# Reordered opening loads, one warm-up moved and a two-piece tail in a fused linear-attention and token-mixing kernel

## The chip, the cores and the metric

The kernel runs on one core of a Trainium2 chip. The metric is the device time of one execution in microseconds, the median of several runs. Engines are named as in the profile: PE is the matmul engine and PEld its weight loads, DVE the vector engine, ACT the scalar engine, POOL the GpSimd engine, SP the engine that issues most transfers. A transfer (DMA) is issued by SP, ACT or POOL into that engine's own queue.

## The reference

Two branches over the same `x` of 2048 rows (S) by 512 columns (D), mixed by a gate per row. `_A_ref` is linear attention with 32 heads of 16 columns, `_B_ref` an MLP over the rows (tokens).

```python
g = sigmoid((x * gate_w).sum(-1))
# A: linear attention
q, k, v = split(x @ wqkv)                      # heads of 16
pq, pk = phi(q), phi(k)                        # phi(t) = where(t > 0, t + 1, exp(t)) + 1e-6
kv = pk^T v ; z = sum_s pk                     # per head
a = ((pq kv) / (pq z + 1e-6)) @ wo
# B: MLP across tokens
h = layernorm(x)
u = gelu(einsum("bsd,sf->bdf", h, w1) + b1)    # F = 1792
b = (u @ w2 + b2)^T
out = g * a + (1 - g) * b
```

Inputs and output are bf16.

## The kernel before

The 2048 rows are 16 tiles of 128 (index `t`), the 512 columns 4 chunks of 128 (index `k` or `j`), F is 14 blocks of 128. `xs` holds x as it is, `xT` its transpose, `wk_sb` the key part of `wqkv` as 4 chunks of 128 rows, each 128 KB. The schedule is manual: each engine executes its instructions in the order of the program text, so the text's order is the queue's order on every engine.

The stages, in order:

- **Opening.** The loads of x tile 0, x tile 1 and the four chunks of Wk are issued, three on SP and two on ACT. Behind them SP issues transposing loads that fill `xT` for the tiles from 2 on, then x, Wq, W1, Wv, Wo. Meanwhile PE runs `warm_up(6)`: six matmuls of 512 columns on a constant, into a bank `wps` that nobody reads. For tiles 0 and 1 (`HEADS = 2`) the transpose is made on PE: `transpose_part` multiplies 128x128 pieces of `xs` by the identity into a bank `pt`, and `copy_part` copies them to `xT` on DVE (line 205 of the profile) or ACT (line 203). Each tile has three parts: chunk 0, chunk 1, chunks 2 and 3. `k_part(t, ks)` then adds steps `ks` of the four accumulation steps of K for tile t, into the bank `kacc`; step k needs `xT` chunk k of that tile and Wk chunk k. PE's order is: transposes of tile 0, steps 0 and 1 of tile 0, transposes of tile 1, step 2 of tile 0, steps 0 and 1 of tile 1, step 3 of tile 0, steps 2 and 3 of tile 1.
- **K loop.** For tiles 2 to 15: four `kacc` steps, `phi` (ACT exp at line 209, DVE at 210 and 213) into `pk`, and with a lag of 4 tiles the Gram products `gacc` (`x^T pk`). Layer-norm statistics run beside it.
- **Q and first W1 blocks.** 16 rounds of three `uacc` matmuls (line 110, as for all matmuls) with the first W1 chunk `w1c[0]`, and one `q_block` of four.
- **Rest of W1.** 11 more F blocks, 16 matmuls each, with gelu; small matmuls for kv and W2; normalisation of q on DVE.
- **Output loop.** For each row tile, 4 `aps` matmuls and 14 `yps` matmuls over the F blocks, one ACT scaling (line 488), one DVE combination (line 501) into `ot`, and a store (line 505). The last row tile is cut by columns into pieces of 256, 128 and 128, each with its own 14 matmuls, combination and store.

The code of the opening's loads and of the tail:

Of the kernel before, what the change touches and what calls it, by code (L numbers as in the profile page):

```python
# [15 lines left out]
def kernel(  # L16
# [13 lines left out]
    nc = tc.nc  # L30
    P = nc.NUM_PARTITIONS
# [6 lines left out]
    S, D = X.shape  # L38
    F = B_w1.shape[1]
    NT = S // P  # L40
# [16 lines left out]
    w1_view = B_w1.rearrange("(t p) f -> p t f", p=P)  # L57
# [11 lines left out]
    def bank(name, dtype=FP32):  # L69
        return ps.tile([P, SC], dtype, name=name, tag="bank")  # L70
# [38 lines left out]
    def mm(o, lhsT, rhs, start, stop, **kw):  # L109
        nc.tensor.matmul(o, lhsT=lhsT, rhs=rhs, start=start, stop=stop, **kw)  # L110
# [14 lines left out]
    def load_x(q, t0, n):  # L125
        q.dma_start(out=xs[:, t0 : t0 + n, :], in_=x_view[:, t0 : t0 + n, :])

    def load_wk(q, k, n):
        q.dma_start(out=wk_sb[:, k : k + n, :], in_=wqkv_view[:, k : k + n, D : 2 * D])
# [4 lines left out]
        )  # L134

    load_x(nc.sync, 0, 1)
    load_wk(nc.scalar, 0, 2)
    load_x(nc.sync, 1, 1)
    load_wk(nc.scalar, 2, 1)
    load_wk(nc.sync, 3, 1)  # L140
    for t in (2, 3, 4):
        load_xT(t, 1)
    nc.vector.memset(ones_f[:], 1.0)
# [3 lines left out]
        out=ident[:], in_=ident[:], compare_op=ALU.not_equal, fill=1.0, base=0,  # L147
# [5 lines left out]
        out=maskQ[:], in_=maskH[:].rearrange("p (a m) -> p m a", m=2), op=ALU.max, axis=AX.X  # L153
# [12 lines left out]
    for c, (j0, nb) in enumerate(w1_chunks):  # L166
        w = wpool.tile([P, NT, FB * P], BF16, name="w1c", tag="wc")
        w1c.append(w)
        nc.sync.dma_start(out=w[:, :, : nb * P], in_=w1_view[:, :, j0 * P : (j0 + nb) * P])
        if c == 0:  # L170
            nc.sync.dma_start(out=wv_sb[:], in_=wqkv_view[:, :, 2 * D : 3 * D])
            nc.sync.dma_start(out=wo_sb[:], in_=wo_view)
# [11 lines left out]
    def warm_up(n, cols=SC):  # L184
        for _ in range(n):
            mm(wps[:, :cols], warm[:, 0:P], warm[:, :cols], True, True)

    act_warm = keep([P, 1], FP32, "act_warm")
    nc.scalar.activation(out=act_warm[:], in_=ones_f[:], func=ACT.Exp)
    warm_up(6)  # L190

    pts = {}

    def transpose_part(t, k0, k1):
        pt = pts[t, k0, k1] = bank("pt")
        for k in range(k0, k1):
            mm(pt[:, k * P : (k + 1) * P], xs[:, t, k * P : (k + 1) * P], ident[:], True, True)

    def copy_part(t, k0, k1, on_act):
        src = pts.pop((t, k0, k1))[:, k0 * P : k1 * P].rearrange("p (k s) -> p k s", k=k1 - k0)  # L200
        dst = xT[:, k0:k1, t * P : (t + 1) * P]
        if on_act:
            nc.scalar.activation(out=dst, in_=src, func=ACT.Copy)
        else:
            nc.vector.tensor_copy(out=dst, in_=src)  # L205
# [13 lines left out]
    def k_part(t, ks):  # L219
        if t not in kaccs:  # L220
            kaccs[t] = bank("kacc")
        for k in ks:
            mm(
                kaccs[t][:], xT[:, k, t * P : (t + 1) * P], wk_sb[:, k, :],
                k == 0, k == ND - 1,
            )

    def k_phi(t):
        phi(pk[:, t, :], kaccs.pop(t))
# [52 lines left out]
    for t in range(HEADS):  # L282
        for k0, k1 in ((0, 1), (1, 2), (2, ND)):
            transpose_part(t, k0, k1)
            copy_part(t, k0, k1, (t, k0) in ((0, 2), (1, 1)))
        k_part(0, range(2) if t == 0 else (2,))
    k_part(1, range(2))
    k_part(0, (3,))
    k_phi(0)
    k_part(1, range(2, ND))  # L290
    k_phi(1)
# [91 lines left out]
    def den_block(c, j):  # L383
        seg = pqT[:, j, c * SC : (c + 1) * SC]
        pz = work.tile([P, SC], FP32, name="pz", tag="pz", bufs=2)
        nc.scalar.activation(out=pz[:], in_=seg, func=ACT.Copy, scale=zcol[:, j : j + 1])  # L386
        nc.vector.transpose(out=zT[:], in_=pz[:])  # L387
        den = work.tile([P, SC // HEAD], FP32, name="den", tag="den", bufs=1)
        nc.vector.tensor_reduce(  # L389
            out=den[:], in_=zT[:].rearrange("p (a d) -> p a d", d=HEAD), op=ALU.add, axis=AX.X  # L390
        )
        rd = work.tile([P, SC // HEAD], BF16, name="rd", tag="rd", bufs=1)
        with nc.allow_low_precision(reason="the normalizer is used in bf16"):
            nc.vector.reciprocal(out=rd[:], in_=den[:])
        rex = work.tile([P, SC], BF16, name="rex", tag="rex", bufs=1)
        nc.vector.transpose(  # L396
            out=rex[:].rearrange("p (a d) -> p a d", d=HEAD),
            in_=rd[:].unsqueeze(2).to_broadcast([P, SC // HEAD, HEAD]),
        )
        nc.vector.tensor_tensor(out=seg, in0=seg, in1=rex[:], op=ALU.mult)  # L400
# [42 lines left out]
    for j in range(NB0, NF):  # L443
        c, jj = divmod(j, FB)
        i = j - NB0
        acc = bank("uacc")
        for t in range(NT):
            if i == 2 and t < BRIDGE:
                for q in range(0, P, Q32):
                    c0 = jj * P + q  # L450
# [24 lines left out]
        out=gg[:], in0=gth[:], scalar1=0.5, scalar2=0.5, op0=ALU.mult, op1=ALU.add  # L475
    )
    nc.vector.tensor_scalar(
        out=c1[:], in0=gth[:], scalar1=-0.5, scalar2=0.5, op0=ALU.mult, op1=ALU.add
# [3 lines left out]
    for t in range(NT):  # L482
        c, tl = divmod(t, TPC)
        aps = bank("aps")
        for j in range(ND):
            mm(aps[:], pqT[:, j, t * P : (t + 1) * P], W2sb[:, j, :], j == 0, j == ND - 1)
        a_sc = work.tile([P, D], FP32, name="a_sc", tag="a_sc", bufs=2)
        nc.scalar.activation(  # L488
            out=a_sc[:], in_=aps[:], func=ACT.Identity,
            scale=gg[:, t : t + 1], bias=c2[:, t : t + 1],  # L490
        )
        for c0, W in ((0, 2 * P), (2 * P, P), (3 * P, P)) if t == NT - 1 else ((0, D),):
            cs = slice(c0, c0 + W)
            yps = bank("yps")
            for f in range(NF):
                mm(
                    yps[:, :W], w2c[c][:, f, tl * P : (tl + 1) * P], uT[:, f, cs],
                    f == 0, f == NF - 1,
                )
            ot = opool.tile([P, D], BF16, name="ot", tag="ot")  # L500
            nc.vector.scalar_tensor_tensor(  # L501
                out=ot[:, :W], in0=yps[:, :W], scalar=c1[:, t : t + 1], in1=a_sc[:, cs],
                op0=ALU.mult, op1=ALU.add,
            )
            (nc.scalar if t < 2 else nc.sync).dma_start(out=o_view[:, t, cs], in_=ot[:, :W])
        if t < NSC * ND - NDB:
            den_block(*divmod(t + NDB, ND))
# [30 lines left out]
```

## Time and profile before

| | |
|---|---|
| runs, us | 162.9, 163.17, 162.28 (median 162.9) |
| profiled execution, us | 162.26, its span 160.6 |
| PE busy | 155.9 us (97%), 822 matmuls |
| DVE busy | 124.3 us (77%) |
| ACT busy | 72.7 us (45%) |
| PE clock granted | 1.0 |
| HBM read, written | 19.01 MB, 2.10 MB |
| first matmul, first K matmul, last DVE combination | 0.85, 4.06, 157.82 us |

The span runs from the first to the last instruction; the execution's own time lies 1.66 us above it. Times inside the execution are in us from the span's start, durations of one instruction in ns. Matmuls are pipelined: one of 512 columns is shown as 379 ns, but a new one starts every 0.216 us. A busy share is an average over stages, and a wait is put down to what came last.

### The profile page before, as it was taken

To read this page: it belongs to the slowest core of one execution; us is meant where nothing else is said; L and a number is where in the kernel's file an instruction comes from. 1 tells how busy PE (TensorE), PEld (TensorE's weight loads), DVE (VectorE), ACT (ScalarE), POOL (GpSimd) and SP (SyncE) were. 2 spreads that over 40 slices of the span, in tenths; PEclk is the share of its full clock that TensorE was granted. 3 is DMA by queue.
4 is the path that set the end of the run, shared out by engine and by line. 5 is a ranking of instruction groups with operands and counts; after the bars stand their busy time and mean duration, and the time that the engine had idled before them with its cause. 6 is when DMAs were issued, how large, how long until landed. Compare 5 with 4: busy or idle time off the path is not lost.

```text
span 160.6 us, 2228 instructions
## 1 busy us (share of the span) xinstructions
PE 155.9 (97%) x822; PEld 72.5 (45%) x836; DVE 124.3 (77%) x274; ACT 72.7 (45%) x113; POOL 7.3 (5%) x17
## 2 busy tenths in 40 slices
PE   7999999999999999999999999999999999999993
PEld 2444444444444445444444444444444444444462
DVE  1599999769999998756999999676999999711122
ACT  3543486654978393059873320237333442111110
POOL 3000332002010000000000000000000000000000
PEclk9999999999999999999999999999999999999999
DMA  5699999999970007600930679401000001110001
GB/s 168 150 231 262 328 352 329 354 349 348 336 171 0 0 0 257 204 0 4 356 101 2 213 244 306 151 33 37 33 33 33 33 33 58 48 61 33 33 33 33
DMA packets 29929, 23.07 MB, mean 144 GB/s; under 512 B 8384, under 2 KB 29888, under 8 KB 29920
## 3 DMA queue, kind: packets, MB, share of 16 engines
q1 hardware_dynamic: 29104, 22.15, 45.2%
q10 hardware_dynamic: 704, 0.66, 1.2%
q0 software_dynamic: 112, 0.14, 0.4%
q8 instruction: 6, 0.10, 0.3%
q14 instruction: 3, 0.02, 0.0%
HBM read 19.01 MB, written 2.10 MB: 131 GB/s over the span
## 4 chain that ended last, share of the span: by engine, by line
PE 84%; DVE 13%; issue 1%; ACT 0%
PE yps L110 30%; PE uacc L110 24%; PE kacc L110 9%; PE gacc L110 9%; PE aps L110 9%; DVE pqT L213 6%; DVE zacc L274 3%; DVE stats L233 2%; DVE e L210 2%; PE wps L110 2%; PE qacc L110 1%; DVE mv L234 1%; ACT e L209 0%; PE kvps L110 0%; PE w2ps L110 0%
## 5 line engine op out<-in xcount | busy, mean ns | idle before, releaser
L110 PE MATMUL uacc<-hs,w1c 128*128 128x512 bf16 (+1 forms) x227 | 50.8, 379 | 0.4 <-issue 0.2
L110 PE MATMUL yps<-uT,w2c 128*128 128x512 bf16 (+2 forms) x247 | 50.8, 355 | 0.3
L110 PEld LDWEIGHTS <-w2c 128*128 128x128 bf16 x252 | 23.6, 98 | 25.2
L110 PEld LDWEIGHTS <-w1c 128*128 128x128 bf16 (+1 forms) x233 | 21.8, 98 | 26.0 <-issue 0.2
L488 ACT ACTIVATE a_sc<-aps,c,gg 128x512 f32<-128x512 f32 x16 | 12.4, 775 | 31.2 <-PE aps L110 15.5
L501 DVE SCALAR_TENSOR_TENSOR ot<-yps,c,a_sc 128x512 bf16<-128x512 f32 (+2 forms) x18 | 12.3, 688 | 15.3 <-PE yps L110 11.7
L322 ACT ACTIVATE uT<-uacc,bcol 128x512 bf16<-128x512 f32 x14 | 9.3, 686 | 17.5 <-PE uacc L110 17.4
L110 PE MATMUL qacc<-xT,wq_sb 128*128 128x512 bf16 x64 | 16.4, 379 | 0.1
L110 PE MATMUL aps<-W2sb,pqT 128*128 128x512 bf16 x63 | 16.4, 379 | 0.1
L110 PE MATMUL kacc<-wk_sb,xT 128*128 128x512 bf16 x63 | 15.9, 379 | 0.2 <-DVE xT L205 0.2
L387 DVE STREAM_TRANSPOSE zT<-pz 128x512 f32<-128x512 f32 x16 | 11.3, 705 | 6.0 <-ACT pz L386 6.0
L110 PE MATMUL gacc<-pk,xs 128*128 128x512 bf16 x63 | 15.7, 379 | 0.1
L249 ACT ACTIVATE hs<-xs,nmr,rstd 128x512 bf16<-128x512 bf16 x16 | 12.8, 805 | 2.3 <-DVE nmr L243 2.3
L209 ACT ACTIVATE e<-kacc 128x512 bf16<-128x512 f32 x16 | 9.4, 594 | 9.7 <-PE kacc L110 8.5
L386 ACT ACTIVATE pz<-pqT,zcol 128x512 f32<-128x512 bf16 x16 | 11.4, 715 | 4.8 <-DVE ot L501 4.7
L209 ACT ACTIVATE e<-qacc 128x512 bf16<-128x512 f32 x16 | 9.5, 594 | 7.7 <-PE qacc L110 7.7
L396 DVE STREAM_TRANSPOSE rex<-rd 128x512 bf16<-128x512 bf16 x16 | 11.4, 711 | 0.6
L213 DVE SCALAR_TENSOR_TENSOR pqT<-qacc,e 128x512 bf16<-128x512 f32 x16 | 11.1, 692 | 0.6
L213 DVE SCALAR_TENSOR_TENSOR pk<-kacc,e 128x512 bf16<-128x512 f32 x16 | 11.1, 692 | 0.6
L389 DVE TENSOR_REDUCE den<-zT 128x32 f32<-128x512 f32 x16 | 11.0, 686 | 0.6
L210 DVE TENSOR_SCALAR e<-e 128x512 bf16<-128x512 bf16 x32 | 9.0, 282 | 2.5 <-ACT e L209 2.5
L233 DVE BATCH_NORM_STATS2 stats<-xs 128x6 f32<-128x512 bf16 x16 | 10.9, 683 | 0.0
(58 smaller groups left out, 96.2 us busy)
## 6 DMA issues: line engine op xcount, KB each, us to landing
w2c<-in_B_w_dram SPq DMA_DIRECT2D x8, 896.0 KB, 5.7
w1c<-in_B_w_dram SPq DMA_DIRECT2D x3, 2048.0 KB, 14.0
out_dram<-ot SPq DMA_DIRECT2D x13, 128.0 KB, 1.7
xs<-in_A_x_dram SPq DMA_DIRECT2D x1, 1024.0 KB, 6.6
w1c<-in_B_w_dram SPq DMA_DIRECT2D x1, 1024.0 KB, 15.3
xs<-in_A_x_dram SPq DMA_DIRECT2D x1, 512.0 KB, 5.0
wq_sb<-in_A_wqkv_dram SPq DMA_DIRECT2D x1, 512.0 KB, 5.6
wv_sb<-in_A_wqkv_dram SPq DMA_DIRECT2D x1, 512.0 KB, 12.3
```

The source lines that it names most:

```text
L110: nc.tensor.matmul(o, lhsT=lhsT, rhs=rhs, start=start, stop=stop, **kw)
L209: nc.scalar.activation(out=e[:], in_=acc[:], func=ACT.Exp)
L210: nc.vector.tensor_scalar(out=e[:], in0=e[:], scalar1=1.0, scalar2=PHI_EPS, op0=ALU.min, op1=ALU.add)
L213: nc.vector.scalar_tensor_tensor(out=dst, in0=acc[:], scalar=0.0, in1=e[:], op0=ALU.max, op1=ALU.add)
L233: nc.vector.bn_stats(out=stats[:], in_=xs[:, t, :])
L249: nc.scalar.activation(out=hs[:, t, :], in_=xs[:, t, :], func=ACT.Identity, scale=rstd[:, t : t + 1], bias=nmr[:, t : t + 1],)
L386: nc.scalar.activation(out=pz[:], in_=seg, func=ACT.Copy, scale=zcol[:, j : j + 1])
L387: nc.vector.transpose(out=zT[:], in_=pz[:])
L389: nc.vector.tensor_reduce(out=den[:], in_=zT[:].rearrange("p (a d) -> p a d", d=HEAD), op=ALU.add, axis=AX.X)
L396: nc.vector.transpose(out=rex[:].rearrange("p (a d) -> p a d", d=HEAD), in_=rd[:].unsqueeze(2).to_broadcast([P, SC // HEAD, HEAD]),)
L488: nc.scalar.activation(out=a_sc[:], in_=aps[:], func=ACT.Identity, scale=gg[:, t : t + 1], bias=c2[:, t : t + 1],)
L501: nc.vector.scalar_tensor_tensor(out=ot[:, :W], in0=yps[:, :W], scalar=c1[:, t : t + 1], in1=a_sc[:, cs], op0=ALU.mult, op1=ALU.add,)
```

## The change

There are three edits.

In the opening, the same five loads are issued in the same places, with other contents. SP sends x tile 0, Wk chunk 0 and x tile 1 (before: x tile 0, x tile 1, Wk chunk 3). ACT sends Wk chunks 1 and 2 together and then chunk 3 (before: chunks 0 and 1 together, then chunk 2). PE runs five warm-ups instead of six, and one of 256 columns behind the transposes of tile 0. Its order then is: transposes of tile 0, the short warm-up, steps 0 to 2 of tile 0, transposes of tile 1, step 3 of tile 0, steps 0 and 1 of tile 1, and steps 2 and 3 of tile 1.

The load of the first W1 chunk, 2 MB, is issued as two transfers of 1 MB, row tiles 0 to 7 and 8 to 15.

The last row tile is cut into 384 and 128 columns, two pieces instead of three.

```diff
     load_x(nc.sync, 0, 1)
-    load_wk(nc.scalar, 0, 2)
+    load_wk(nc.scalar, 1, 2)
+    load_wk(nc.sync, 0, 1)
+    load_wk(nc.scalar, 3, 1)
     load_x(nc.sync, 1, 1)
-    load_wk(nc.scalar, 2, 1)
-    load_wk(nc.sync, 3, 1)
     for t in (2, 3, 4):
         load_xT(t, 1)
...
-        nc.sync.dma_start(out=w[:, :, : nb * P], in_=w1_view[:, :, j0 * P : (j0 + nb) * P])
+        for t0, t1 in ((0, NT // 2), (NT // 2, NT)) if c == 0 else ((0, NT),):
+            nc.sync.dma_start(
+                out=w[:, t0:t1, : nb * P], in_=w1_view[:, t0:t1, j0 * P : (j0 + nb) * P]
+            )
...
-    warm_up(6)
+    warm_up(5)
...
             copy_part(t, k0, k1, (t, k0) in ((0, 2), (1, 1)))
-        k_part(0, range(2) if t == 0 else (2,))
+        if t == 0:
+            warm_up(1, 256)
+            k_part(0, range(3))
+    k_part(0, (3,))
     k_part(1, range(2))
-    k_part(0, (3,))
     k_phi(0)
...
-        for c0, W in ((0, 2 * P), (2 * P, P), (3 * P, P)) if t == NT - 1 else ((0, D),):
+        for c0, W in ((0, 3 * P), (3 * P, P)) if t == NT - 1 else ((0, D),):
```

## The prediction

> **What bounds the kernel now.** I read the waits of the matmul engine first, for all of the execution (columns: waited in total, times, longest).
>
> ```profile
> PE wps L110 <- PEq L522: 0.8, 1, 0.8
> PE kacc L110 <- DVE xT L205: 0.2, 1, 0.2
> PE uacc L110 <- issue: 0.2, 1, 0.2
> ```
>
> PE waits for the program's start, once in the opening, once for nothing visible. The busy time by stretch agrees (length, then busy time and instructions of PE, PEld, DVE, ACT, POOL, then clock and DMA):
>
> ```profile
> 5.20:32.20 27.00, 26.89 (x124) 12.27 (x126) 23.88 (x60) 14.91 (x25) 3.82 (x5) 1.00 1.03 289
> 32.20:56.50 24.30, 24.14 (x112) 11.03 (x113) 22.29 (x53) 15.52 (x26) 2.08 (x2) 1.00 0.66 198
> ```
>
> The second row settles a doubt. The page's chain runs through DVE there (13% of the span), but 112 matmuls of 512 columns at 0.216 us (kacc: four in 0.86) are 24.2 of its 24.3 us. So from about 5.1 to 157.8 us PE is gapless, and what the opening gives or loses reaches the end unchanged. Only the opening and the tail can move the time. The chain of the opening, start and length:
>
> ```profile
> 0.85 2.72 PE wps L110 x6
> 3.57 0.12 PE pt L110
> 3.69 0.02 issue
> 3.71 0.30 DVE xT L205
> 4.01 0.05 issue
> 4.06 0.60 PE kacc L110 x2
> 4.66 0.22 PE pt L110 x4
> 4.89 0.22 PE kacc L110
> 5.10 0.00 issue
> 5.11 1.04 PE kacc L110 x4
> ```
>
> Six warm-ups (wps), the transposes of x tile 0 (pt, in truth from 3.36), the copy of their first part, two steps of kacc 0, the transposes of tile 1, the third step, and then kacc 1 at 5.11, after which nothing stops. Kacc 0 still owes its fourth step there. Count both programs to the same state, kacc 0 complete and kacc 1 not begun: before, 5.11 + 0.216 = 5.33.
>
> What the loads allow is in the DMA issues (KB each, us to landing):
>
> ```profile
> xs<-in_A_x_dram SPq DMA_DIRECT2D x2, 128.0 KB, 2.7
> wk_sb<-in_A_wqkv_dram ACTq DMA_DIRECT2D x1, 256.0 KB, 3.1
> wk_sb<-in_A_wqkv_dram ACTq DMA_DIRECT2D x1, 128.0 KB, 3.3
> wk_sb<-in_A_wqkv_dram SPq DMA_DIRECT2D x1, 128.0 KB, 3.3
> ```
>
> The 2.7 is a mean: asked for separately, the two x tiles take 2.3 and 3.0. SP issues at 0.81, 1.27, 1.73 and ACT at 0.81, 1.30. Landings by place: SP first 3.11, second 4.27, third 5.03; ACT's pair 3.91, its second 4.60.
>
> **The opening's loads.** The sizes by place do not change: SP sends 128, 128, 128 KB, ACT 256 and 128, the same number of issues in the same slots; the xT transposes stay behind SP's third. Only the contents change. I therefore keep the landing of each place:
> - Wk chunk 0: 3.91 becomes 4.27 (SP second).
> - Chunks 1 and 2: 3.91 (chunk 2 was 4.60). Chunk 3: 4.60 (was 5.03).
> - x tile 1: 4.27 becomes 5.03 (SP third).
>
> The Wk chunks 2 and 3 that come earlier were not waited for (their matmuls started at 4.72 and about 5.5). The two that come later are the ones PE needs first. So the reorder buys nothing by these rows and makes two arrivals late. The main unknown is x tile 1 in third place: no row shows an x tile there. From below: as early as now, 4.27. From above: 5.3, the 5.03 of the Wk chunk plus the 0.3 between the landing times of 3.0 and 3.3. I take 5.03, since bytes and place are those of that row.
>
> [...]
>
> **Five warm-ups.** Warm-ups start at 0.85, 1.23, 1.65, 2.08, 2.50 and 2.93; the sixth holds PE until 3.36, although the weights of the first transpose were let go by x's landing at 3.19:
>
> ```profile
> 3.19 0.32 PEld L110 LDWEIGHTS <-xs 128*128 128x128 bf16 x2 [0.53 <-DMA xs<-in_A_x_dram]
> ```
>
> With five, PE is free at 2.93 and the transposes start at about 3.22 (weights to matmul 0.03, as in the first warm-up). That is 0.14 earlier, so the first copy ends at 3.87 and kacc 0 could start at 3.92. It can't: chunk 0 lands at 4.27. The 0.14 is lost behind that wait.
>
> **The one later warm-up**, 256 columns, comes after the transposes: 0.11 us at the fast pitch, 0.21 at the slow one (half of 0.216 and of 0.427). It ends by 3.9, covered by the wait until 4.32. Were the chunk there at once, it would cost at most 0.1.
>
> **Running it forward.** Landing to start took 0.05 to 0.08. Three steps run from 4.32 to 4.97. Tile 1's transposes wait for x: 5.03 + 0.06 = 5.09, end 5.31; queued behind them on PE are step 3 of kacc 0 (5.31 to 5.53) and all of kacc 1. The way from tile 1's first transpose to the first matmul of kacc 1 was 4.50 to 5.11, 0.61 (transpose, copy, wake), so kacc 1 starts at 5.70. The common state comes at 5.70 against 5.33: **+0.37**. The bounds give: x at 4.27 with the chunk at 4.27, transposes at 4.97, kacc 1 at 5.58, +0.25; x at 5.3, +0.64. Running step 3 before kacc 1 saves nothing: it fills time spent waiting for the copies. phi of tile 0 can start a little earlier, off the path.
>
> **W1's first chunk in two halves.** One more SP issue, 0.52 long by the row of the chunk now (issued at 18.25). The queue behind it is Wv, Wo and the later W1 chunks. The first chunk landed 11.3 after issue, 29.6, and is first read at 31.9, margin 2.3; the same packets are moved. Cost 0; if that margin were gone, 0.5 at most.
>
> **The tail.** The end of the chain, and the last DVE evictions by shape (busy, mean ns, idle before):
>
> ```profile
> 154.69 3.10 PE yps L110 x42
> 157.82 0.35 DVE ot L501
> ```
> ```profile
> L501 DVE SCALAR_TENSOR_TENSOR ot<-yps,c,a_sc 128x512 bf16<-128x512 f32 x2 | 1.5, 752 | 6.3 <-PE yps L110 6.3
> L501 DVE SCALAR_TENSOR_TENSOR ot<-yps,c,a_sc 128x128 bf16<-128x128 f32 x2 | 0.7, 351 | 0.7 <-PE yps L110 0.7
> L501 DVE SCALAR_TENSOR_TENSOR ot<-yps,c,a_sc 128x256 bf16<-128x256 f32 x1 | 0.5, 484 | 1.6 <-PE yps L110 1.6
> ```
>
> A whole row tile is 14 matmuls, 3.02; in three pieces 42, 3.10. So 28 more cost 0.08, and 14 fewer give back **0.04**. The eviction of 384 columns is an estimate between 484 and 752 ns, 0.62: from 157.02 (where the second piece's began, 157.04, less 0.02) to 157.64, before the last piece is ready at 157.78. SP's issue of it takes 0.33 and is over by 158.0, before the last issue at 158.16. Bounds: if the 96 KB store sits in the way of the last 32 KB one, up to 0.1 more; nothing shows a gain above 0.1.
>
> **The sum.** +0.37 - 0.04 = +0.33. On the profiled execution (162.26, span 160.6) that is 162.6. That execution is among the fastest; the median of the three runs is 162.9, so **163.2**.
>
> **Rivals.**
>
> *The clock step comes late (slower).* The matmuls begin at half speed: warm-ups 0.427 apart, later kacc steps 0.216. The first transpose is still slow (314 ns), the next ones 219, so the step is near 3.45, 2.6 us after the first matmul. The change leaves PE idle from 2.93 to 3.22, just ahead of it, and again until 4.32. If the step needs that 2.6 us of work unbroken, it comes at 4.32 + 2.6 = 6.9. Then three steps end at 5.60, tile 1's transposes at 6.03, step 3 at 6.46 and one step of kacc 1 at 6.89, a state that before had at 5.54: +1.35, minus the tail, 164.2. It decides as soon as the lost 0.43 us of work matters; added up without regard to gaps, 2.6 us of work are there at about 3.7, under the wait, at no cost. For it: this is what the sixth warm-up may have been buying. Against: a gap of 0.4 us after the step (3.69 to 4.06) did not undo it.
>
> [...]
>
> *Transfers land by size (faster).* If chunk 0 lands before 3.9 and x tile 1 by 4.3, three steps run from 3.92 to 4.57 and kacc 1 starts at 5.18: -0.15, with the tail -0.2, 162.7. Against: both queues share the same rate then (about 380 GB/s from 3.0 to 4.1).
>
> *It all hides.* If in most runs the step to the fast clock comes after 4.3, both openings are clock-bound and the extra waits are partly covered: about +0.1, 163.0.
>
> **How the numbers follow.** About 0.5%, 0.8 us, is what a measurement of this kernel can tell from no change. Late x tile 1, with the hidden case: 0.60, at 163.0 to 163.4. Late clock step: 0.23, at 164.2. Landing by size: 0.17, at 162.7. No case gains 0.8; the three runs lie 0.9 apart, and that spread alone gives faster 0.10. Slower by over 0.8: nearly all of the clock case, and the upper bound of x's landing (+0.64 before spread), 0.30. Same, 0.60. The range takes in the size case less some spread, 162.5, and the clock case, 164.3.
>
> **What would show it.** Right: the first kacc matmul near 4.3 and waiting for Wk's DMA, tile 1's transposes near 5.1 and waiting for x's DMA, kacc 1 near 5.7, then no waits; 28 yps matmuls in about 3.06. The clock rival: kacc matmuls 0.43 apart beyond 4.3. Wrong: kacc 1 before 5.11, an x tile landing under 4.6 in third place, or any new wait of PE after 6 us.

## The result and the profile after

The changed kernel takes 163.38 us (median of 22 runs, 162.64 to 165.13) against 162.9 (22 runs, 162.25 to 163.34). The ratio is 1.0036, 95% interval [1.0019, 1.0053]: 0.36% slower. The interval leaves out 1, so the change costs something, less than the 0.5% that the prediction took a measurement to tell apart. The forecast was 163.2, from 162.5 to 164.3. The profiled execution took 162.64, span 160.9, against 162.26 and 160.6; 162.6 was forecast for it. (Runs more than 1.5% above the fastest are left out of the ratios, here after's two at 165.1 and one of 165.22 later; they stay in the medians, ranges and counts.)

The two kernels also differ in spread: 2.5 us after, 1.1 before. One profile can't show that; the experiments do.

The waits of PE over the whole execution, after (waited in total, times, longest):

```profile
PE wps L110 <- PEq L527: 0.8, 1, 0.8
PE kacc L110 <- DMA wk_sb<-in_A_wqkv_dram: 0.4, 1, 0.4
```

The wait for DVE's copy has given way to one for a Wk load. The third wait of before, 0.2 us for "issue" ahead of a `uacc` step, is no wait of the program: there two matmuls start 0.43 us apart, twice the usual 0.216, and such pairs recur every 10.8 us or so in before's trace, which holds 227 `uacc` records where after's holds 233. Single records are missing there. The chain of the opening, after (start, length):

```profile
1.26 3.02 DMA wk_sb<-in_A_wqkv_dram
4.28 0.04 issue
4.32 0.81 PE kacc L110 x3
5.13 0.35 PE pt L110 x4
5.48 3.63 PE kacc L110 x16
```

It now begins with a transfer: chunk 0, issued second on SP at 1.26, lands at 4.28, and three steps of kacc 0 run from 4.32. The timeline of the same stretch shows the second late arrival (start, length, engine, line, operation; in brackets the idle time before and its cause):

```profile
3.06 0.61 PE L110 MATMUL pt<-ident,xs 128*128 128x128 bf16 x4
3.47 0.42 PE L110 MATMUL wps<-const-bfloat16-1.0 128*128 128x256 bf16 x1
5.08 0.23 PEld L110 LDWEIGHTS <-xs 128*128 128x128 bf16 x4 [0.44 <-DMA xs<-in_A_x_dram]
5.70 0.13 PEld L110 LDWEIGHTS <-xT 128*128 128x128 bf16 x2 [0.34 <-DVE xT L208]
```

The transposes of tile 0 begin 0.3 earlier than before, the short warm-up follows, and PE stands idle until chunk 0 is there. Tile 1's weights wait for x until 5.08, and kacc 1 starts at 5.70, against 5.11 with one step owed.

At the other end, the chain of the tail, after:

```profile
155.07 3.07 PE yps L110 x28
158.14 0.03 issue
158.17 0.35 DVE ot L506
```

28 matmuls in 3.07 instead of 42 in 3.10. The last combination starts 0.35 later than before (157.82).

The traces say how much of that lies between opening and tail. The first Gram product (`gacc`) starts at 8.79 before and at 9.16 after, 0.38 later. From there to the start of the last matmul it takes 148.78 us before and 148.74 after. All fourteen profiles of this document have one of two lengths there: 148.78 with the tail in three pieces, 148.74 to 148.75 with two. So what sets the kernels apart lies ahead of the first Gram product or behind the last matmul, and nothing between adds to it.

### The profile page after: what moved, and what is told of

It reads as the page before. It is cut to its first block, busy times and chain, and to the rows that moved or that the text cites. A ratio compares the mean times of both kernels' runs of the same rounds, so it can differ in the third digit from the quotient of the medians.

```text
span 160.9 us, 2212 instructions
## 1 busy us (share of the span) xinstructions
PE 156.8 (97%) x822; PEld 71.5 (44%) x822; DVE 124.1 (77%) x273; ACT 72.9 (45%) x113; POOL 7.3 (5%) x17
## 4 chain that ended last, share of the span: by engine, by line
PE 96%; DMA 2%; SPq 0%; DVE 0%; issue 0%
PE uacc L110 30%; PE yps L110 30%; PE kacc L110 9%; PE qacc L110 9%; PE gacc L110 9%; PE aps L110 9%; DMA wk_sb<-in_A_wqkv_dram 2%; PE kvps L110 0%; SPq L126 0%; PE w2ps L110 0%; DVE ot L506 0%; PE pt L110 0%; PE pt L333 0%
## 5 line engine op out<-in xcount | busy, mean ns | idle before, releaser
L110 PE MATMUL uacc<-hs,w1c 128*128 128x512 bf16 (+1 forms) x233 | 51.5, 379 | 0.0
L110 PEld LDWEIGHTS <-w2c 128*128 128x128 bf16 x238 | 22.8, 98 | 25.9
L110 PEld LDWEIGHTS <-xs 128*128 128x128 bf16 x72 | 6.8, 100 | 8.8 <-DMA xs<-in_A_x_dram 1.3
```

## The experiments

All times are medians, with the fastest and slowest run, against runs of the kernel before on the same chip (median 162.7 to 162.8, slowest 163.45).

Two theories stood against each other. Theory 1: the loads, by their new places, cost some 0.4 us in every run, and the thinner opening lets PE's step to full speed come late in some runs. Rival: the spread comes from the landings in their new places.

**Six warm-ups again, none behind the transposes** (kernel `a_six`, from after).

```diff
-    warm_up(5)
+    warm_up(6)
...
-            warm_up(1, 256)
```

> The kernel after with six full warm-ups ahead of the transposes and none behind them. Theory 1 (late x tile 1 sets the best time, the missing warm-up sets the spread): fastest run as after, about 162.6, since x tile 1 still lands near 5.03; the runs spread no wider than before's 1.1 us, so none above 163.9 and a median near 163.2. Rival (the spread of after comes from the landings in their new places): fastest 162.6, but runs up to 165 as after, median 163.4 or more.

163.42 (162.8 to 163.6, 12 runs), ratio 1.0031 [1.0014, 1.0047]. The spread fell to 0.8 and nothing lies above 163.6, but the median is 0.2 over what was expected.

**More warm-ups under the wait** (`a_fill`, from after).

```diff
-            warm_up(1, 256)
+            warm_up(3, 256)
```

> The kernel after with three short warm-ups (256 columns) behind tile 0's transposes instead of one, so that PE works from 3.06 to about 4.1 us, all of it under the wait for Wk chunk 0 until 4.32. Theory 1: the gap ahead of the clock step is gone, the spread falls to before's, highest run below 163.9, median near 163.1, fastest 162.6. Rival (landings): as after, runs up to 165. Rival (the sixth warm-up's place, ahead of the transposes, is what matters): as after.

163.31 (162.67 to 163.58, 12 runs), ratio 1.0019 [1.0004, 1.0035]. Two more matmuls that compute nothing, in time that PE would have waited, removed every run above 163.6. (At after's rate, 12 runs of 34 above 163.7 with the second measurement below, twelve runs without one have a chance of 0.5%.) The loads and their places are after's, so the rival falls. The median missed: 0.2 over the 163.1 expected.

**Five warm-ups alone** (`b_five`, from before).

```diff
-    warm_up(6)
+    warm_up(5)
```

> The kernel before with five warm-ups instead of six, nothing else. Theory 1: fastest run 0.1 below before's (transposes at 3.1 instead of 3.36, kacc 0 then held by the Wk pair's landing at 3.91, kacc 1 at about 5.0), but a thinner opening: some runs 1.3 to 2.5 us above the fastest, as in after. Rival (landings make the spread): spread as before, 1.1 us, median 0.1 below before's.

162.65 (162.21 to 163.24, 12 runs), ratio 0.9998 [0.998, 1.0016]. A miss for theory 1 as first put: a gap ahead of the transposes alone makes no high runs. The fastest run gained 0.07.

**The new loads alone** (`b_newloads`: the kernel before with the change's load order, six warm-ups, PE's order of before).

```diff
-    load_wk(nc.scalar, 0, 2)
+    load_wk(nc.scalar, 1, 2)
+    load_wk(nc.sync, 0, 1)
+    load_wk(nc.scalar, 3, 1)
     load_x(nc.sync, 1, 1)
-    load_wk(nc.scalar, 2, 1)
-    load_wk(nc.sync, 3, 1)
```

> The kernel before with only the five loads in the changed order; six warm-ups and PE's order as before. Theory 1: x tile 1 lands at 5.03, transposes at 5.09, kacc 1 at 5.70 with step 3 of kacc 0 still owed: +0.59 on the fastest run (162.85), spread as before, median about 163.5. Rival (it is the order of PE, not the loads, that costs): within 0.1 of before. Rival (landings make the spread): runs up to 165.

163.15 (162.89 to 163.53, 12 runs), ratio 1.0024 [1.001, 1.0037]. The fastest run is 0.61 above before's 162.28, where 0.59 was worked out. So in their best runs the loads cost what their places say, and the change's PE order gives part of that back. The median missed: it is 0.34 above before's, where some 0.6 (163.5) was expected. That the cost shrinks when both kernels are still at half speed, as the table below suggests, would explain it; it wasn't tested apart.

**The change with the old loads** (`a_oldloads`: the same lines of the loads, turned back, in the kernel after).

> The kernel after with the five loads put back as in before; its PE order, its five warm-ups and one later, its tail and the split W1 load stay. Theory 1: chunk 2 lands at 4.60 and holds step 2 of kacc 0, the transposes of tile 1 queue behind it at 4.87, kacc 1 starts at 5.48 with kacc 0 complete: +0.15, less 0.04 of the tail, +0.11 on the fastest run; so some two thirds of the cost is the loads. Rival (PE's order alone costs it): +0.3, as after.

162.72 (162.37 to 163.41, 12 runs), ratio 1.0000 [0.9984, 1.0016]. The fastest run is 0.14 above before's 162.23, 0.11 expected. Putting the loads back undoes the loss in the median, and the high runs are gone too.

**The kernel after once more** (`after_again`, no edit).

> The kernel after, unchanged, measured again beside the others of this call. Theory 1 (the thinner opening lets the clock step come very late in some runs): some of the runs lie above 163.9, up to 165, as in the first measurement, fastest 162.6, median 163.4. Rival (those high runs came from the chip or the hour, not from the kernel): no run above 163.7, median 163.3, as the three kernels with the same loads that were just measured.

163.49 (162.73 to 165.22, 12 runs), ratio 1.0036 [1.0014, 1.0059]. Five of twelve runs are above 163.7, where 7 of the first 22 were: 12 of 34. (The 14 of a later expectation counts 163.67 and 163.70 too.) The high runs belong to the kernel. And its profiled execution, 164.27, is one of them. The timeline of its opening:

```profile
3.43 0.61 PE L110 MATMUL pt<-ident,xs 128*128 128x128 bf16 x4 [0.29 <-DMA xs<-in_A_x_dram]
3.83 0.42 PE L110 MATMUL wps<-const-bfloat16-1.0 128*128 128x256 bf16 x1
4.56 1.44 PE L110 MATMUL kacc<-wk_sb,xT 128*128 128x512 bf16 x3 [0.31 <-DMA wk_sb<-in_A_wqkv_dram]
5.79 0.63 PE L110 MATMUL pt<-ident,xs 128*128 128x128 bf16 x4
6.22 4.09 PE L110 MATMUL kacc<-wk_sb,xT 128*128 128x512 bf16 x14
```

Three steps take 1.44 here, 0.81 in the first profile. The groups by shape, from 4 to 8 us, the first line of after, the second of this run (busy us, mean ns, idle before):

```profile
L110 PE MATMUL kacc<-wk_sb,xT 128*128 128x512 bf16 x15 | 3.7, 379 | 0.4 <-DMA wk_sb<-in_A_wqkv_dram 0.4
```
```profile
L110 PE MATMUL kacc<-wk_sb,xT 128*128 128x512 bf16 x8 | 3.6, 602 | 0.3 <-DMA wk_sb<-in_A_wqkv_dram 0.3
```

In the same time 8 steps instead of 15, at 602 ns instead of 379: PE ran at half speed until about 8.05.

**Fewer warm-ups, old loads** (`b_four`, from before), and **no late warm-up** (`a_nolater`, from after). If the idle time before the step counts, wherever it lies, `b_four` must show high runs without any load moved, and `a_nolater` more than after.

```diff
-    warm_up(6)
+    warm_up(4)
```

> The kernel before with four warm-ups instead of six, loads and order as before. Sharpened theory 1: what matters is how long PE stands idle in all before the step, not where. Profiles so far put that idle time after the first matmul at 0.98 us in the run of after that was slow (step near 7.8), and at 0.4 to 0.75 in kernels whose runs all stayed below 163.7. With four warm-ups it is 0.5 to 0.9 ahead of the transposes and 0.3 behind, 0.8 to 1.2: some runs above 163.7 and up to 165, though no load is moved. Rival (the new place of Wk chunk 0 makes the step come late): no run above 163.5, as with five.

163.75 (163.34 to 164.43, 6 runs), ratio 1.0073 [1.0046, 1.0101]; three of six above 163.7. Not the loads: the idle time.

```diff
-            warm_up(1, 256)
```

> The kernel after without the one short warm-up behind tile 0's transposes, so five and no more. Sharpened theory 1: 0.2 us more idle time ahead of the step than after, 1.0 to 1.3: at least as many runs above 163.7 as after (14 of 34), likely more than half, fastest 162.6, median 163.7. Rival (the short warm-up does nothing): as after, median 163.4. Rival (it costs, as work queued ahead of kacc 0): faster than after.

164.56 (162.82 to 165.09, 7 runs), ratio 1.0096 [1.006, 1.0131]; six of seven above 163.7, and the median 0.9 over what was expected. One matmul of 256 columns, 0.21 us, was worth about one microsecond of the median.

**The tail and the split, together and apart** (`b_tail_split`, `b_tail`, `b_split`, each the kernel before with those edits of the change).

> The kernel before with the two-piece tail and the split W1 load only. All theories: the last 14 matmuls fewer give 0.04 us, the split nothing; median within 0.1 of before. Rival (the 96 KB store holds up the last 32 KB one): up to 0.1 slower.

162.73 (162.52 to 163.45), ratio 1.0013 [0.9994, 1.0032]. The fastest run was 0.3 above before's, so the two were run apart.

> The kernel before with only the tail changed to 384 + 128 columns. Theory: 14 matmuls fewer, 0.04 us less by the profile; times within 0.1 of before. Rival (the larger store, or something else about the tail, costs 0.2, which the tail and split together looked like): fastest near 162.5, median near 162.95.

162.87 (162.47 to 163.48), ratio 1.0007 [0.9989, 1.0026].

> The kernel before with only the first W1 chunk loaded in two halves. Theory: it lands over 2 us before it is read, times within 0.1 of before. Rival (one more transfer issued costs 0.2 somewhere): fastest near 162.5, median near 162.95.

163.06 (162.56 to 163.62), ratio 1.0017 [0.9998, 1.0036]. Each interval holds 1, so neither edit has a cost that these runs show, though the split's reaches 0.36%. The profiles tell more. From the first Gram product to the last matmul, the stretch in which the halves of W1 land and are read, `b_split` takes the 148.78 us of before, so the split costs PE nothing. What does vary is the end: from the start of the last combination to the end of the execution it is 4.43 to 4.45 us in before, `b_five`, `b_four` and `b_newloads`, but 4.74 in `b_split`, 4.63 in `b_tail` and 4.71 in `c_best` below. It isn't the split, since after, with the same split, has 4.47; what holds the end up in those three is not shown. The tail's own term is seen in the profile of `b_tail`:

```profile
154.81 3.07 PE yps L110 x28
157.88 0.02 issue
157.90 0.35 DVE ot L501
```

PE is done with the tail 0.03 sooner in two pieces. But with two pieces the way from the last combination to the end takes 4.46 to 4.50 us in after, `after_again`, `a_fill`, `a_six`, `a_nolater`, `a_oldloads` and `b_tail_split`, some 0.03 more than with three, so nothing of the gain is left at the end.

**A candidate** (`c_best`: the loads and PE order of before, tail of after, and the warm-ups below).

```diff
-    warm_up(6)
+    warm_up(5)
+    warm_up(1, 256)
...
+        if t == 0:
+            warm_up(1, 256)
         k_part(0, range(2) if t == 0 else (2,))
```

> A candidate: the loads and PE's order of before, five and a half warm-ups ahead of the transposes (five of 512 columns and one of 256, PE free near 3.15), one of 256 columns behind tile 0's transposes, and the tail of after (384 + 128). Theory 1: kacc 0 is held by the Wk pair at about 3.95 to 4.1 instead of 4.06, so at best 0.1 from the opening and 0.04 from the tail: fastest 162.15, median 162.7, spread as before (1.1 us). Rival (x tile 0's landing varies enough to hold the transposes until 3.3 anyway): within 0.05 of before.

162.97 (162.48 to 163.48, 12 runs), ratio 1.0017 [1.0001, 1.0033]: a miss. PE's part came as planned in its profile (the first kacc step at 3.92 instead of 4.06), but the first steps ran at half speed, as the next table shows. Of the 0.55 by which its profiled execution is above before's, 0.28 is there at the start of the last combination (158.10 against 157.82) and 0.27 comes behind it. Why its fastest run is 0.25 above before's is not settled. No version here is shown to beat the kernel before.

**The step in all profiles.** The moment at which the starts of successive matmuls fall from 0.427 to 0.216 apart (for 128 columns, from 0.107 to 0.056), the profiled execution's own time, and how long PE stood idle between its first matmul and the first kacc step (worked out from the starts, each slow 128-column matmul taken as 0.107, a slow 256-column one as 0.213):

| kernel | loads | step at, us | its time, us | idle, us | runs above 163.7 |
|---|---|---|---|---|---|
| before | old | 3.65 | 162.26 | 0.3 | 0 of all |
| b_five | old | 4.3 | 162.38 | 0.77 | 0 of 12 |
| b_tail | old | 4.3 | 162.53 | 0.27 | 0 of 12 |
| b_tail_split | old | 4.8 | 162.63 | 0.32 | 0 of 12 |
| c_best | old | 5.1 | 162.81 | 0.13 | 0 of 12 |
| b_split | old | 5.95 | 163.29 | 0.28 | 0 of 12 |
| a_oldloads | old | 6.8 | 163.41 | 0.39 | 0 of 12 |
| b_four | old | 6.85 | 163.34 | 0.96 | 3 of 6 |
| after | new | 4.07 | 162.64 | 0.77 | 12 of 34, with the next |
| after_again | new | 8.05 | 164.27 | 0.99 | |
| b_newloads | new | 5.75 | 163.2 | 0.74 | 0 of 12 |
| a_fill | new | 6.8 | 163.58 | 0.48 | 0 of 12 |
| a_six | new | 6.8 | 163.6 | 0.65 | 0 of 12 |
| a_nolater | new | 7.1 | 163.78 | 1.20 | 6 of 7 |

The traces of before and after also hold a record of the granted clock. Its full speed begins at 3.65 in before, the moment in the table; in after, where PE stood idle around the step, the moment is taken from there (4.07).

Three readings. With the same loads the time follows the step: from before to `b_four` 1.08 us for 2.8 us more at half speed after the first kacc step (4.06), from after to `after_again` 1.63 for 3.7, both about 0.4 per us; a stretch at half speed costs just under half its length. At about the same step (6.8) the new loads cost 0.2 (163.58 and 163.6 against 163.41 and 163.34), at an early one 0.38. And runs above 163.7 appear only where the idle time came to about 0.8 and more, and grow with it. After lies on that edge. Its work ahead of the first K step is always the same, so its idle time goes by when that step starts, which is when Wk chunk 0 lands: at 4.28 in one profile and 4.52 in the other, and the idle time was 0.77 and 0.99. (x tile 0 came later too, 2.6 us after issue instead of 2.2; that only moved idle time from behind the transposes to ahead of them.)

## Why the prediction was right

**Landings by place: right.** Chunk 0 landed at 4.28 (forecast 4.27), x tile 1 at 5.03 by its 3.3 us from issue (5.03). The transposes of tile 1 started at 5.08 (5.09), kacc 1 at 5.70 (5.70). Both bounds on x tile 1 were not needed: an x tile in third place took what the Wk chunk there had taken. That it agrees to 0.01 is luck in part: in the other profiles with the new loads chunk 0 landed 3.1 to 3.25 us after issue, not 3.0. A chunk of 128 KB alone in second place needed 3.0 us, as x tile 1 had there in before.

**Tile 0's transposes: earlier than forecast.** 3.06 instead of 3.22, as x landed at 3.0 and not at 3.11. It made no difference: hidden behind chunk 0, as forecast.

**The tail: right on PE, nothing in the time.** 0.03 for 0.04 up to the last combination, and as much lost behind it (4.47 us to the end instead of 4.44). Both are beyond what run times can resolve. The split cost PE the 0 that was forecast.

**The sum: right in the best case.** +0.38 on the profiled execution, +0.39 between the fastest runs, against +0.33. By the trace it is 0.38 at the first Gram product, 0.37 forecast. `b_newloads` and `a_oldloads` test the same arithmetic on other orders, 0.61 for 0.59 and 0.14 for 0.11, by their fastest runs alone. What the sum leaves out comes next.

**The clock rival: true at the same time, with the wrong mechanism.** The prediction gave it a chance of 0.23, as if a kernel had it or not. In fact it is in a third of the runs. It is also why the mean moved more than the sum says: 163.55 and 163.60 in the two measurements of after, against 162.83 and 162.72, so 0.7 to 0.9; with the gap filled (`a_fill`) the difference of the means is 0.4. The medians show it less plainly: 0.48 and 0.75 in the two measurements, and still 0.50 with the gap filled, which is not settled. The price has a sound sum in it and some luck. It was for a step at 6.9, counted from the median of 162.9; counted from the profiled 162.26 it gives 163.57, and `a_fill` and `a_six`, with steps at 6.8, took 163.58 and 163.6. That the 164.2 lies next to the 164.27 of `after_again` is chance, since the step came at 8.05 there. The mechanism that priced it, 2.6 us of unbroken work, is refuted: `a_six` worked unbroken from 0.85 to 3.79 and still had its step at 6.8. The 2.6 was a misreading too. Of tile 0's transposes in before the first two are slow (314 ns), the third is 263 and the fourth 219, so the step was at 3.65, not 3.45.

What sets the moment of the step is not shown. It is no property of a kernel: the two profiles of after have it at 4.07 and 8.05, and all fourteen lie from 3.65 to 8.05. Nor does the idle time alone place it: `a_six` had 0.65 us and its step at 6.8, after 0.77 and 4.07. The record of the granted clock shows full speed for 157.01 us from the step in before and in after, and 0.50 behind it (160.7 to 162.5 in before, 161.1 to 162.9 in after).

**"It all hides": half right.** With the step near 6.8 the cost is 0.2, more than the 0.1 put there, less than 0.38.

**Transfers by size: wrong.** No transfer came earlier for being smaller: from issue to landing, SP's second and third places took 3.0 and 3.3 us in both kernels, ACT's two 3.1 and 3.3.

## What to carry to other kernels

Here, reordering loads of like size on two queues permuted the arrival times among the contents (SP's second and third landed at 4.27 and 5.03 before, at 4.28 and 5.03 after). So give the early places to what the bound engine needs first, and check which of the improved arrivals anyone was waiting for. Idle time that looks free because a transfer is awaited can still be paid for later: while PE ran at half speed, one matmul that computes nothing, placed in the wait, was worth more than its length (0.21 us for about one of the median). A kernel's spread over runs is a measurement too; one profile of this change showed only half of what it did.

## What the runs showed of the hardware

The step to full speed came between 3.65 and 8.05 us in kernels that begin much alike, and each us of delay costs about 0.4 us. Four of them have the very opening of before (before, `b_tail`, `b_tail_split`, `b_split`): their steps lie at 3.65, 4.3, 4.8 and 5.95, and their first Gram products at 8.79, 8.90, 9.15 and 9.51. A step that moves to 6.85, as in `b_four`, is worth 1.1 us, as much as the whole spread of the kernel before. The granted clock read 1.00 over 4.3 to 8.0 us in the profile of after and in that of `after_again` alike (stretch, then PE and PEld, clock, DMA share, GB/s):

```profile
4.30:8.00 3.70, 3.67 (x19) 1.58 (x19) 1.00 0.55 120
```
```profile
4.30:8.00 3.70, 3.44 (x12) 1.48 (x12) 1.00 0.65 151
```

19 matmuls against 12 in the same stretch, both at clock 1.00: that column doesn't show the half speed at a kernel's start, and the busy share hardly does. The record of the granted clock holds nothing ahead of the step (its first entry is at 4.07 in after, at 3.65 in before), and there the column reads 1.00, as it does in before from 0.85 to 3.40, with warm-ups 0.427 apart. The state is read from the spacing of the matmuls.
